# Four-byte key transposes, a lighter PE share, a reordered end and longer weight rows in a decode attention kernel

## The chip, the cores and the metric

The kernel runs on one core of a Trainium2 chip. The metric is the device time of one launch in microseconds (us), the median of several runs. Engines are named as in the profile: PE is TensorE (matmul), PEld its weight load, DVE VectorE, ACT ScalarE, SP SyncE, which here only issues DMA. The profile counts 16 DMA engines for the core. "Late engines" below means eight of them, which fall behind the other eight in the course of the run (in the kernel before all sixteen are within 0.6 us at the first load and the two groups some 20 us apart at the end, by the landing marks explained below).

## The reference, cut to what matters

One token passes through attention over a cache of 32768 keys in each of 32 heads of 192 elements, and then through a small MLP. K and V are 403 MB each in bf16. Every byte is used once, so a kernel that is limited only by loading would show nothing but loads.

```python
B, Sq, D = 1, 1, 640
H, Sk, Dh = 32, 32768, 192
...
def reference(A_x, A_k_cache, A_v_cache, A_wq, A_wo, B_x, B_w1, B_w2):
    def _A_ref(x, k_cache, v_cache, wq, wo):
        q = (x @ wq).reshape(B, Sq, H, Dh)                    # (transpose left out)
        scores = jnp.einsum("bhqd,bhkd->bhqk", q, k_cache) * (Dh ** -0.5)
        p = _softmax(scores, axis=-1)
        o = jnp.einsum("bhqk,bhkd->bhqd", p, v_cache)
        return o.reshape(B, Sq, H * Dh) @ wo                  # (transpose left out)
    ...
    h = x + _A_ref(_layernorm(x, axis=-1), A_k_cache, A_v_cache, A_wq, A_wo)
    h2 = h + _B_ref(_layernorm(h, axis=-1), B_w1, B_w2)       # w2 after relu after w1
    return h2
```

## The kernel before

A load brings 64 keys to each of the 128 partitions (3 MB) and is worked in two chunks of 32 keys a partition. Of each chunk, PE scores 20 keys: it transposes them in blocks of 128 bf16 columns, ACT copies the result out of PSUM, and PE multiplies. DVE scores the other 12 with a multiplication and a sum.

```python
full = [(JL, [(J, 20), (J, 20)])] * (Sk // (P * JL))      # JL = 64, J = 32: (keys of a chunk, those that PE scores)
ends = full[:-1] + [(40, [(20, 12), (20, 12)]), (16, [(16, 10)]), (8, [(8, 4)])]   # the last head
...
def transposes(g):
    ...
    for b0 in range(0, NB, 8):
        nb = min(8, NB - b0)
        tp = tps.tile([P, 8, P], bf16, name="tp")
        for b in range(nb):
            off = (c0 + jc - jp) * Dh + (b0 + b) * P
            nc.tensor.transpose(out=tp[:, b, :], in_=kt[:, off:off + P], identity=ident_b[:])   # L239
        nc.scalar.copy(out=kT[:, b0:b0 + nb, :], in_=tp[:, 0:nb, :])                            # L240

def scores_pe(g):          # three matmuls for two keys
    ...
    for i in range(JP // 2):
        nc.tensor.matmul(sp[:, 2 * i:2 * i + 2], lhsT=kT[:, 3 * i + 1, :], rhs=qm[:, 1:3], ...)     # L249
        nc.tensor.matmul(sp[:, 2 * i:2 * i + 1], lhsT=kT[:, 3 * i, :], rhs=qm[:, 0:1], ...)         # L251
        nc.tensor.matmul(sp[:, 2 * i + 1:2 * i + 2], lhsT=kT[:, 3 * i + 2, :], rhs=qm[:, 3:4], ...) # L253

def scores_dve(g):
    ...
    nc.vector.tensor_tensor(out=pr[:, 0:JD, :], in0=kt[...], in1=qb[...], op=A.mult)                # L266
    nc.vector.reduce_sum(out=sc[:, 0:JD], in_=pr[:, 0:JD, :], axis=mybir.AxisListType.X)            # L269
...
# the loop: PE's program order
for g in range(G):
    ...                    # loads of this chunk
    transposes(g)
    if g > 0:
        pv(g - 1)          # the matmuls with V, L293
    scores_pe(g)
    sc = scores_dve(g)
    ...
    exp_dve(g, sc)
den_mm(H - 1)
den_rec(H - 1)
pv(G - 1)
o_scale(H - 1)             # L314 on DVE, L315 on ACT
o_turn(H - 1)              # L327: o by columns, for the projection
project(H // 2 - 1)        # with wo; then layernorm and MLP
```

The softmax here doesn't subtract the row's maximum and nothing guards it: scores larger than these inputs give would overflow.

## Time and profile before

The time is 1954.15 us (1954.13 to 1954.15 in the three runs).

| what | before | where it stands |
|---|---|---|
| span of the profiled run | 1952.3 us | first line of the page |
| DMA engines busy | 99.0% on the data queue | page, part 3 |
| rate in the middle | 429 to 431 GB/s | page, part 2 |
| PE / DVE / ACT busy | 82 / 69 / 55% | page, part 1 |
| instruction packets of queue q8 | 159 | page, part 3 |
| last full K load landed | 1912.1 us | landing marks in the trace |
| last matmul with V ended | 1940.66 us | chain in order of time |

The groups that the change rewrites are these three of part 5. The columns are line, engine, operation, output from input, count, then busy time and mean ns of one, then the idle time ahead of them and its main cause:

```profile
L266 DVE TENSOR_TENSOR pr<-kt,qb 128x2304 f32<-128x2304 bf16 (+1 forms) x258 | 655.0, 2539 | 483.3 <-DMA kt<-in_A_k_cache_dram 479.9
L239 PE MATMUL tp<-ident_b,kt 128*128 128x128 bf16 x7677 | 599.3, 242 | 342.8 <-DMA kt<-in_A_k_cache_dram 269.7
L269 DVE TENSOR_REDUCE sc<-pr 128x12 f32<-128x2304 f32 (+1 forms) x258 | 654.3, 2536 | 27.6 <-ACT kT L240 1.4
```

DVE waits 480 us for K loads and PE 270. That is the picture of a kernel that is limited by its DMA: time taken off a group of 600 us on PE need not save a microsecond.

The other quantity used throughout is not on the page. Each load leaves 16 landing marks in the trace, which I read as one for each DMA engine (the marks carry no engine's number). These are the marks of the last full K load of the kernel before, in us relative to the last of them at 1912.1:

```
-21.7 -21.7 -21.7 -21.5 -21.5 -21.4 -20.4 -17.5 | -1.8 -1.6 -1.5 -1.5 -1.5 -0.5 -0.2 0.0
```

Eight engines are 20 us ahead of the other eight. A load is whole only with the last mark (DVE began on this K at 1912.17, after 4.36 us of waiting for it), so the eight late ones set the pace. Below, "late mean" is the mean of the eight later marks of the last full V load, which follows that K: 1918.5 us before.

### The profile page before, as it was taken

To read this page: it belongs to the slowest core of one execution; us is meant where nothing else is said; L and a number is where in the kernel's file an instruction comes from. 1 tells how busy PE (TensorE), PEld (TensorE's weight loads), DVE (VectorE), ACT (ScalarE), POOL (GpSimd) and SP (SyncE) were. 2 spreads that over 40 slices of the span, in tenths; PEclk is the share of its full clock that TensorE was granted. 3 is DMA by queue.
4 is the path that set the end of the run, shared out by engine and by line. 5 is a ranking of instruction groups with operands and counts; after the bars stand their busy time and mean duration, and the time that the engine had idled before them with its cause. 6 is when DMAs were issued, how large, how long until landed. Compare 5 with 4: busy or idle time off the path is not lost.

```text
span 1952.3 us, 44906 instructions
## 1 busy us (share of the span) xinstructions
PE 1594.4 (82%) x20392; PEld 1122.4 (57%) x20392; DVE 1338.0 (69%) x654; ACT 1067.5 (55%) x2223; POOL 0.7 (0%) x6
## 2 busy tenths in 40 slices
PE   6887887878788788787888877888788887887887
PEld 4655565555556556555555655655555565565655
DVE  5766777667666676676767666777666766676675
ACT  4555555555555555555655555555555555555554
POOL 0000000000000000000000000000000000000000
PEclk9989889989998889998988989899899989898998
DMA  9999999999999999999999999999999999999996
GB/s 405 431 429 429 430 431 430 429 429 431 431 430 428 430 431 430 431 429 431 430 429 430 429 431 430 430 431 424 431 431 428 425 421 431 427 430 426 430 421 253
DMA packets 51522, 827.85 MB, mean 424 GB/s; under 512 B 4612, under 2 KB 17412, under 8 KB 18564
## 3 DMA queue, kind: packets, MB, share of 16 engines
q1 hardware_dynamic: 51332, 824.99, 99.0%
q8 instruction: 159, 2.61, 0.5%
q14 instruction: 31, 0.25, 0.0%
HBM read 824.97 MB, written 0.00 MB: 423 GB/s over the span
## 4 chain that ended last, share of the span: by engine, by line
DMA 77%; PE 17%; ACT 4%; DVE 1%; issue 1%; SPq 0%; ACTq 0%
DMA kt<-in_A_k_cache_dram 75%; PE o_ps L293 8%; PE tp L239 6%; ACT kT L240 3%; DMA vt<-in_A_v_cache_dram 1%; DVE pr L266 1%; PE sp L249 1%; PE sp L253 1%; PE sp L251 1%; PE qps L205 0%; ACT pA L276 0%; ACT pB L256 0%; DVE o_pair L314 0%; PE oT_ps L327 0%; ACT row_e L208 0%
## 5 line engine op out<-in xcount | busy, mean ns | idle before, releaser
L240 ACT COPY kT<-tp 128x1024 bf16<-128x1024 bf16 (+1 forms) x1025 | 905.2, 966 | 343.1 <-PE tp L239 340.2
L266 DVE TENSOR_TENSOR pr<-kt,qb 128x2304 f32<-128x2304 bf16 (+1 forms) x258 | 655.0, 2539 | 483.3 <-DMA kt<-in_A_k_cache_dram 479.9
L239 PE MATMUL tp<-ident_b,kt 128*128 128x128 bf16 x7677 | 599.3, 242 | 342.8 <-DMA kt<-in_A_k_cache_dram 269.7
L239 PEld LDWEIGHTS <-kt 128*128 128x128 bf16 x7677 | 531.1, 110 | 381.2 <-DMA kt<-in_A_k_cache_dram 280.2
L269 DVE TENSOR_REDUCE sc<-pr 128x12 f32<-128x2304 f32 (+1 forms) x258 | 654.3, 2536 | 27.6 <-ACT kT L240 1.4
L293 PE MATMUL o_ps<-vt,pB 128*2 128x384 bf16 x2559 | 498.8, 346 | 2.6 <-DMA vt<-in_A_v_cache_dram 2.6
L293 PEld LDWEIGHTS <-pB 128*2 128x2 bf16 x2559 | 203.8, 87 | 226.9 <-issue 65.9
L256 ACT ACTIVATE pB<-sp 128x20 bf16<-128x20 f32 (+1 forms) x258 | 48.4, 188 | 492.4 <-PE sp L253 492.4
L293 PE MATMUL o_ps<-vt,pA 128*2 128x384 bf16 x1537 | 291.9, 326 | 0.0
L249 PEld LDWEIGHTS <-kT 128*128 128x128 bf16 x2559 | 196.1, 96 | 85.7 <-issue 84.7
L249 PE MATMUL sp<-qm,kT 128*128 128x2 bf16 x2559 | 218.6, 164 | 0.5 <-ACT kT L240 0.5
L251 PE MATMUL sp<-qm,kT 128*128 128x1 bf16 x2559 | 215.0, 163 | 0.0
L253 PE MATMUL sp<-qm,kT 128*128 128x1 bf16 x2559 | 215.0, 163 | 0.0
L251 PEld LDWEIGHTS <-kT 128*128 128x128 bf16 x2559 | 198.7, 96 | 0.0
L293 PEld LDWEIGHTS <-pA 128*2 128x2 bf16 x1537 | 129.1, 84 | 120.8
L253 PEld LDWEIGHTS <-kT 128*128 128x128 bf16 x2559 | 197.4, 96 | 0.0
L276 ACT ACTIVATE pA<-sc 128x12 bf16<-128x12 f32 (+1 forms) x258 | 52.8, 205 | 0.0
L256 ACT ACTIVATION_READ_ACCUMULATOR pB<-sp 128x1 f32 x258 | 50.1, 194 | 0.0
L276 ACT ACTIVATION_READ_ACCUMULATOR pA<-sc 128x1 f32 x258 | 49.3, 191 | 0.0
L305 DVE TENSOR_REDUCE rec<-den 128x1 f32<-128x20 f32 x32 | 5.7, 179 | 60.2 <-PE den L299 60.2
L315 ACT ACTIVATE o_pair<-o_ps,rec 2x192 f32<-2x192 f32 x32 | 13.2, 412 | 26.9 <-DVE o_pair L314 26.9
L327 PE MATMUL oT_ps<-ident_f,o_pair 2*128 2x1 f32 x192 | 24.2, 247 | 0.1
(60 smaller groups left out, 191.4 us busy)
## 6 DMA issues: line engine op xcount, KB each, us to landing
kt<-in_A_k_cache_dram SPq DMA_DIRECT2D x127, 3072.0 KB, 35.7
vt<-in_A_v_cache_dram SPq DMA_DIRECT2D x127, 3072.0 KB, 31.4
wq<-in_A_wq_dram SPq DMA_DIRECT2D x8, 960.0 KB, 34.7
wo<-in_A_wo_dram SPq DMA_DIRECT2D x16, 480.0 KB, 31.2
kt<-in_A_k_cache_dram SPq DMA_DIRECT2D x1, 1920.0 KB, 30.7
vt<-in_A_v_cache_dram SPq DMA_DIRECT2D x1, 1920.0 KB, 25.4
kt<-in_B_w_dram SPq DMA_DIRECT2D x1, 1920.0 KB, 17.1
vt<-in_B_w_dram SPq DMA_DIRECT2D x2, 960.0 KB, 13.3
```

Of the source, the lines that this page charges most:

```text
L239: nc.tensor.transpose(out=tp[:, b, :], in_=kt[:, off:off + P], identity=ident_b[:])
L240: nc.scalar.copy(out=kT[:, b0:b0 + nb, :], in_=tp[:, 0:nb, :])
L249: nc.tensor.matmul(sp[:, 2 * i:2 * i + 2], lhsT=kT[:, 3 * i + 1, :], rhs=qm[:, 1:3], start=True, stop=False, skip_group_check=True)
L251: nc.tensor.matmul(sp[:, 2 * i:2 * i + 1], lhsT=kT[:, 3 * i, :], rhs=qm[:, 0:1], start=False, stop=False, skip_group_check=True)
L253: nc.tensor.matmul(sp[:, 2 * i + 1:2 * i + 2], lhsT=kT[:, 3 * i + 2, :], rhs=qm[:, 3:4], start=False, stop=True, skip_group_check=True)
L256: nc.scalar.activation(out=pB[:, 0:JP], in_=sp[:, 0:JP], func=F.Exp, scale=SCALE, accum_out=dsums[:, h, 2 * c + 1:2 * c + 2])
L266: nc.vector.tensor_tensor(out=pr[:, 0:JD, :], in0=kt[:, c0 * Dh:(c0 + JD) * Dh].rearrange("p (j d) -> p j d", d=Dh), in1=qb[:].unsqueeze(1 ...
L269: nc.vector.reduce_sum(out=sc[:, 0:JD], in_=pr[:, 0:JD, :], axis=mybir.AxisListType.X)
L276: nc.scalar.activation(out=pA[:, 0:JD], in_=sc[:, 0:JD], func=F.Exp, scale=SCALE, accum_out=dsums[:, h, 2 * c:2 * c + 1])
L293: nc.tensor.matmul(o[:], lhsT=p, rhs=vt[:, (c0 + j) * Dh:(c0 + j + 2) * Dh], start=first, stop=last)
L315: nc.scalar.activation(out=dst[:, 1, n0:n0 + Dh], in_=o[:, Dh:2 * Dh], func=F.Copy, scale=s[0:2, 1:2])
L327: nc.tensor.matmul(ps[:, b:b + 1], lhsT=src[:, i, b * P:(b + 1) * P], rhs=ident_f[0:2, i:i + 1], start=(i == 0), stop=(i == 1))
```

## The change

The intent has four parts. (1) Two neighbouring bf16 elements are taken as one 4-byte word, so that one transpose moves 256 columns; the scores then use every second element of the transposed block as weights, even and odd parity in turn. (2) PE scores 20 and 16 keys of the two chunks in turns, and DVE 12 and 16. (3) At the end all K pieces are scored ahead of the V work that waits for data. (4) The rows of wo are loaded as 3840 B instead of 1280 B, and o is written in a permuted order to suit. Cut to its core:

```diff
-    full = [(JL, [(J, 20), (J, 20)])] * (Sk // (P * JL))
-    ends = full[:-1] + [(40, [(20, 12), (20, 12)]), (16, [(16, 10)]), (8, [(8, 4)])]
+    full = [(JL, [(J, 20), (J, 16)])] * (Sk // (P * JL))
+    ends = full[:-1] + [(40, [(20, 12), (20, 12)]), (16, [(16, 8)]), (8, [(8, 4)])]
...
-    wo_view = A_wo.rearrange("(b p) n -> p b n", p=P)
+    wo_view = A_wo.rearrange("(g p b) n -> g p b n", p=P, b=3)
...          # V pieces of the end: one DMA for each chunk; qm of 12 columns, by block and parity
-                tp = tps.tile([P, 8, P], bf16, name="tp")
+                tp = tps.tile([P, 4, P], f32, name="tp")
                 for b in range(nb):
-                    off = (c0 + jc - jp) * Dh + (b0 + b) * P
-                    nc.tensor.transpose(out=tp[:, b, :], in_=kt[:, off:off + P], identity=ident_b[:])
-                nc.scalar.copy(out=kT[:, b0:b0 + nb, :], in_=tp[:, 0:nb, :])
+                    off = (c0 + jc - jp) * Dh + (b0 + b) * 2 * P
+                    nc.tensor.transpose(out=tp[:, b, :], in_=kt[:, off:off + 2 * P].bitcast(f32), identity=ident_f[:])
+                nc.scalar.copy(out=kT[:, b0:b0 + nb, :], in_=tp[:, 0:nb, :].bitcast(bf16))
...
-            for i in range(JP // 2):
-                ...                                            # three matmuls for two keys
+            for i in range(JP // 4):
+                for b in range(3):
+                    for e in range(2):
+                        nc.tensor.matmul(sp[:, 4 * i + b:4 * i + b + 2], lhsT=kT[:, 3 * i + b, e:2 * P:2],
+                                         rhs=qm[:, 4 * b + 2 * e:4 * b + 2 * e + 2], ...)
...          # scores_dve: more than 12 keys are done in pieces
+            n = -(-JD // JDM)
+            for j0, j1 in [(JD * i // n, JD * (i + 1) // n) for i in range(n)]:
...          # o_scale: the same two instructions with a permuted output
+            dst = o_pair[(h // 2) % 2][:].rearrange("q i (b p) -> q i p b", b=3)
+            nc.vector.tensor_scalar_mul(out=dst[:, 0, p0:p1, :], in0=src[:, 0], scalar1=s[0:2, 1:2])
+            nc.scalar.activation(out=dst[:, 1, p0:p1, :], in_=src[:, 1], func=F.Copy, scale=s[0:2, 1:2])
...          # the end, behind the loop over the full chunks
+        transposes(ENDS[0])
+        pv(ENDS[0] - 1)
+        sc = scores_dve(ENDS[0])
+        for i, g in enumerate(ENDS[1:]):
+            transposes(g)
+            scores_pe(g - 1)
+            exp_dve(g - 1, sc)
+            sc = scores_dve(g)
+            if i > 0:
+                pv(g - 2)
+        scores_pe(G - 1)
+        exp_dve(G - 1, sc)
         den_mm(H - 1)
         den_rec(H - 1)
+        pv(G - 2)
         pv(G - 1)
```

More of the change, by code (lines that the diff above doesn't have):

```diff
@@ L65 @@
     G = len(chunks)
+    ENDS = [g for g in range(G) if chunks[g][2] >= len(loads) - NEND]
     NCH = [sum(1 for q in chunks if q[0] == h) for h in range(H)]
     NCM = max(NCH)
-    NBM = max(q[5] for q in chunks) * Dh // P
-    JDM = max(q[4] - q[5] for q in chunks)
+    NBM = max(q[5] for q in chunks) * Dh // (2 * P)
+    JDM = 12
     const = ctx.enter_context(tc.tile_pool(name="const", bufs=1))
@@ L79 @@
     scp = ctx.enter_context(tc.tile_pool(name="scp", bufs=3))
-    pcp = ctx.enter_context(tc.tile_pool(name="pcp", bufs=3))
+    pcp = ctx.enter_context(tc.tile_pool(name="pcp", bufs=6))
     small = ctx.enter_context(tc.tile_pool(name="small", bufs=2))
@@ L112, in load_wo, with load_part @@
         t = wop.tile([P, 3, D], bf16, name="wo")
-        nc.sync.dma_start(out=t[:], in_=wo_view[:, 3 * pr:3 * pr + 3, :])
+        nc.sync.dma_start(out=t[:], in_=wo_view[pr])
         wo_t[pr] = t
-    def load_part(ld, src, pool, tag, name):
+    def load_part(ld, src, pool, tag, name, parts=None):
         h, k0, jl = loads[ld]
@@ L122, in load_part @@
         t = pool.tile([P, size], bf16, tag=tag, name=name)
-        nc.sync.dma_start(out=t[:, 0:jl * Dh], in_=src[h, k0:k0 + P * jl, :].rearrange("(p j) d -> p (j d)", p=P))
+        rows = src[h, k0:k0 + P * jl, :].rearrange("(p j) d -> p (j d)", p=P)
+        for j0, j1 in parts or [(0, jl)]:
+            nc.sync.dma_start(out=t[:, j0 * Dh:j1 * Dh], in_=rows[:, j0 * Dh:j1 * Dh])
         return t
@@ L129, in load_v @@
     def load_v(ld):
-        vt_t[ld] = load_part(ld, v_hd, vpool, "vt", "vt")
+        parts = [(q[3], q[3] + q[4]) for q in chunks if q[2] == ld] if ld >= len(loads) - NEND else None
+        vt_t[ld] = load_part(ld, v_hd, vpool, "vt", "vt", parts)
     w_t = {}
@@ L157 @@
     nc.vector.memset(eps_t[:], eps)
-    rows_e = [const.tile([1, 4 * P], bf16, name=f"row_e{i}") for i in range(2)]
+    rows_e = [const.tile([1, 3 * Dh], bf16, name=f"row_e{i}") for i in range(2)]
     for r in rows_e:
@@ L207, in q_rows @@
             r = rows_e[h % 2]
-            nc.scalar.copy(out=r[0:1, 0:Dh], in_=qps[:])
-            nc.scalar.copy(out=r[0:1, 4 * P - Dh:4 * P], in_=qps[:])
+            nc.scalar.copy(out=r[0:1, Dh:2 * Dh], in_=qps[:])
         def q_spread(h):
             r = rows_e[h % 2]
-            qbps = mm_bank([P, Dh + 4], f32, "qbps")
-            nc.tensor.matmul(qbps[:, 0:Dh], lhsT=ones_row[:], rhs=r[0:1, 0:Dh], start=True, stop=True)
-            for i in range(4):
-                nc.tensor.matmul(qbps[:, Dh + i:Dh + i + 1], lhsT=r[0:1, i * P:(i + 1) * P],
-                                 rhs=ones_row[0:1, 0:1], start=True, stop=True)
+            qbps = mm_bank([P, Dh + 12], f32, "qbps")
+            nc.tensor.matmul(qbps[:, 0:Dh], lhsT=ones_row[:], rhs=r[0:1, Dh:2 * Dh], start=True, stop=True)
+            i = Dh
+            for b in range(3):
+                for e in range(2):
+                    for off in ((1 - 0) * Dh + b * (2 * P - Dh), b * (2 * P - Dh)):
+                        nc.tensor.matmul(qbps[:, i:i + 1], lhsT=r[0:1, off + e:off + 2 * P:2],
+                                         rhs=ones_row[0:1, 0:1], start=True, stop=True)
+                        i += 1
             qb = qbp.tile([P, Dh], bf16, name="qb")
             nc.scalar.copy(out=qb[:], in_=qbps[:, 0:Dh])
-            qm = qbp.tile([P, 4], bf16, name="qm")
-            nc.scalar.copy(out=qm[:], in_=qbps[:, Dh:Dh + 4])
+            qm = qbp.tile([P, 12], bf16, name="qm")
+            nc.scalar.copy(out=qm[:], in_=qbps[:, Dh:Dh + 12])
             qb_t[h], qm_t[h] = qb, qm
@@ L231, in transposes @@
             kt = kt_t[ld]
-            NB = jp * Dh // P
-            kT = tsb.tile([P, NBM, P], bf16, name="kT")
-            for b0 in range(0, NB, 8):
-                nb = min(8, NB - b0)
-                tp = tps.tile([P, 8, P], bf16, name="tp")
+            NB = jp * Dh // (2 * P)
+            kT = tsb.tile([P, NBM, 2 * P], bf16, name="kT")
+            for b0 in range(0, NB, 4):
+                nb = min(4, NB - b0)
+                tp = tps.tile([P, 4, P], f32, name="tp")
                 for b in range(nb):
-                    off = (c0 + jc - jp) * Dh + (b0 + b) * P
-                    nc.tensor.transpose(out=tp[:, b, :], in_=kt[:, off:off + P], identity=ident_b[:])
-                nc.scalar.copy(out=kT[:, b0:b0 + nb, :], in_=tp[:, 0:nb, :])
+                    off = (c0 + jc - jp) * Dh + (b0 + b) * 2 * P
+                    nc.tensor.transpose(out=tp[:, b, :], in_=kt[:, off:off + 2 * P].bitcast(f32), identity=ident_f[:])
+                nc.scalar.copy(out=kT[:, b0:b0 + nb, :], in_=tp[:, 0:nb, :].bitcast(bf16))
             kT_t[g] = kT
@@ L247, in scores_pe @@
             sp = sps.tile([P, J], f32, name="sp")
-            for i in range(JP // 2):
-                nc.tensor.matmul(sp[:, 2 * i:2 * i + 2], lhsT=kT[:, 3 * i + 1, :], rhs=qm[:, 1:3],
-                                 start=True, stop=False, skip_group_check=True)
-                nc.tensor.matmul(sp[:, 2 * i:2 * i + 1], lhsT=kT[:, 3 * i, :], rhs=qm[:, 0:1],
-                                 start=False, stop=False, skip_group_check=True)
-                nc.tensor.matmul(sp[:, 2 * i + 1:2 * i + 2], lhsT=kT[:, 3 * i + 2, :], rhs=qm[:, 3:4],
-                                 start=False, stop=True, skip_group_check=True)
+            for i in range(JP // 4):
+                for b in range(3):
+                    for e in range(2):
+                        nc.tensor.matmul(sp[:, 4 * i + b:4 * i + b + 2], lhsT=kT[:, 3 * i + b, e:2 * P:2],
+                                         rhs=qm[:, 4 * b + 2 * e:4 * b + 2 * e + 2],
+                                         start=(i == 0 and b == 0 and e == 0),
+                                         stop=(i == JP // 4 - 1 and b == 2 and e == 1), skip_group_check=True)
             pB = pcp.tile([P, J], bf16, name="pB")
@@ L264, in scores_dve @@
             qb = qb_t[h]
-            pr = prp.tile([P, JDM, Dh], f32, name="pr")
-            nc.vector.tensor_tensor(out=pr[:, 0:JD, :], in0=kt[:, c0 * Dh:(c0 + JD) * Dh].rearrange("p (j d) -> p j d", d=Dh),
-                                    in1=qb[:].unsqueeze(1).to_broadcast([P, JD, Dh]), op=A.mult)
             sc = scp.tile([P, J], f32, name="sc")
-            nc.vector.reduce_sum(out=sc[:, 0:JD], in_=pr[:, 0:JD, :], axis=mybir.AxisListType.X)
+            n = -(-JD // JDM)
+            for j0, j1 in [(JD * i // n, JD * (i + 1) // n) for i in range(n)]:
+                pr = prp.tile([P, JDM, Dh], f32, name="pr")
+                nc.vector.tensor_tensor(out=pr[:, 0:j1 - j0, :],
+                                        in0=kt[:, (c0 + j0) * Dh:(c0 + j1) * Dh].rearrange("p (j d) -> p j d", d=Dh),
+                                        in1=qb[:].unsqueeze(1).to_broadcast([P, j1 - j0, Dh]), op=A.mult)
+                nc.vector.reduce_sum(out=sc[:, j0:j1], in_=pr[:, 0:j1 - j0, :], axis=mybir.AxisListType.X)
             return sc
@@ L311, in o_scale @@
             o = o_t.pop(h)
-            dst = o_pair[(h // 2) % 2]
-            n0 = (h % 2) * Dh
-            nc.vector.tensor_scalar_mul(out=dst[:, 0, n0:n0 + Dh], in0=o[:, 0:Dh], scalar1=s[0:2, 1:2])
-            nc.scalar.activation(out=dst[:, 1, n0:n0 + Dh], in_=o[:, Dh:2 * Dh], func=F.Copy, scale=s[0:2, 1:2])
+            dst = o_pair[(h // 2) % 2][:].rearrange("q i (b p) -> q i p b", b=3)
+            p0, p1 = (h % 2) * Dh // 3, (h % 2 + 1) * Dh // 3
+            src = o[:].rearrange("q (i p b) -> q i p b", i=2, b=3)
+            nc.vector.tensor_scalar_mul(out=dst[:, 0, p0:p1, :], in0=src[:, 0], scalar1=s[0:2, 1:2])
+            nc.scalar.activation(out=dst[:, 1, p0:p1, :], in_=src[:, 1], func=F.Copy, scale=s[0:2, 1:2])
         oT_t = {}
@@ L344 @@
         q_spread(0)
-        for g in range(G):
+        for g in range(ENDS[0]):
             h, c, ld, c0, jc, jp = chunks[g]
-            end = ld - (len(loads) - NEND)
-            if end == 0 and c0 == 0:
-                for i in range(NEND):
-                    load_k(ld + i)
-                for i in range(NEND):
-                    load_v(ld + i)
-                load_w("w1", B_w1, kpool, "kt", 1)
-                load_w("w2", B_w2, vpool, "vt", 2)
-            elif end < 0 and c0 == 0 and g > 0:
+            if c0 == 0 and g > 0:
                 load_k(ld)
@@ L380 @@
             exp_dve(g, sc)
+        for ld in range(len(loads) - NEND, len(loads)):
+            load_k(ld)
+        for ld in range(len(loads) - NEND, len(loads)):
+            load_v(ld)
+        load_w("w1", B_w1, kpool, "kt", 1)
+        load_w("w2", B_w2, vpool, "vt", 2)
+        transposes(ENDS[0])
[10 more added lines that the diff above has]
+        exp_dve(G - 1, sc)
         den_mm(H - 1)
         den_rec(H - 1)
+        pv(G - 2)
         pv(G - 1)
```

## The prediction

> **What bounds the kernel now.** I read the page first: parts 1 to 3, then the chain of part 4.
>
> ```profile
> span 1952.3 us, 44906 instructions
> PE 1594.4 (82%) x20392; PEld 1122.4 (57%) x20392; DVE 1338.0 (69%) x654; ACT 1067.5 (55%) x2223; POOL 0.7 (0%) x6
> ...
> q1 hardware_dynamic: 51332, 824.99, 99.0%
> q8 instruction: 159, 2.61, 0.5%
> ...
> DMA 77%; PE 17%; ACT 4%; DVE 1%; issue 1%; SPq 0%; ACTq 0%
> DMA kt<-in_A_k_cache_dram 75%; PE o_ps L293 8%; PE tp L239 6%; ACT kT L240 3%; DMA vt<-in_A_v_cache_dram 1%; DVE pr L266 1%; PE sp L249 1%; PE sp L253 1%; PE sp L251 1%; PE qps L205 0%; ACT pA L276 0%; ACT pB L256 0%; DVE o_pair L314 0%; PE oT_ps L327 0%; ACT row_e L208 0%
> ```
>
> The reader is to see that the 16 DMA engines are busy for the whole span, that no compute engine is, and that the chain is mostly K loads. A pair of loads (K and V, 6.29 MB) takes 14.6 us at the 431 GB/s of the middle slices; PE is busy 12.2 us of it, DVE 10.4. So nearly all the compute that the change touches is hidden.
>
> The share of 99% hides one thing. The trace also holds the 16 landing marks of each load, one per DMA engine. Sorted, they fall into two groups of eight: the first load lands within 0.6 us, the one that is whole at 882 us has eight engines 13 us ahead, from 1400 us on about 20 us ahead. Up to 1250 us the gap between the two groups grows by 0.175 us for each packet of the queue "instruction" (a straight-line fit of the gap against the count of such packets). The reading that fits is that instruction fetches run on the late eight engines only, and one 16 KB fetch costs its engine 8 x 0.175 = 1.4 us (the packet itself took 0.93 us). The 159 fetches then cost 27.8 us, and they are on the path: a load has landed only when its late engines have. [...]
>
> Next the end, from the chain in order of time and the DVE timeline:
>
> ```profile
> 1906.10 25.42 DMA vt<-in_A_v_cache_dram
> ...
> 1939.51 0.40 PE den L299 x2
> 1939.91 0.75 PE o_ps L293 x4
> 1940.68 0.42 DVE o_pair L314
> ...
> 1949.51 0.39 PE ytp L408
> ```
>
> ```profile
> 1912.17 2.56 DVE L266 TENSOR_TENSOR pr<-kt,qb 128x2304 f32<-128x2304 bf16 x1 [4.36 <-DMA kt<-in_A_k_cache_dram]
> 1914.83 2.55 DVE L269 TENSOR_REDUCE sc<-pr 128x12 f32<-128x2304 f32 x1
> ...
> 1924.21 1.76 DVE L266 TENSOR_TENSOR pr<-kt,qb 128x1536 f32<-128x1536 bf16 x1 [1.57 <-DMA kt<-in_A_k_cache_dram]
> 1926.07 1.75 DVE L269 TENSOR_REDUCE sc<-pr 128x8 f32<-128x1536 f32 x1
> ...
> 1935.42 0.95 DVE L269 TENSOR_REDUCE sc<-pr 128x4 f32<-128x768 f32 x1
> ```
>
> The first V of the end lands at 1931.5. Until then PE stands at L293, in program order, with scores behind it that need no V; 9.2 us of PE work follow to the end of the last L293 at 1940.66, and 11.6 us of projection and MLP follow that. By the landing marks the late engines never pause: last full K 1912.1, its V 1919.4, end K pieces 1924.1 to 1927, V 1931.5 to 1934.4, w1 1939.1, w2 1944.0.
>
> [...] the one f32 transpose (L408, 128 columns) is one pass of 0.38 us, begun at 1949.51 at a half clock and read by DVE at 1949.92[...] f32 loads of 128 columns take 187 ns and start 0.11 us apart, bf16 ones 0.056 us apart among the transposes.
>
> **The change, part by part.**
>
> *Transposes.* 7677 bf16 become 3456 f32 (half as many blocks, 18 PE keys in place of 20 on average). For a pair: before 60 x 0.056 = 3.4 us, after 27 x 0.112 to 0.17 = 3.0 to 4.6 us. *Scores*: 54 matmuls for 60; with every second word as weights I take 25 to 50 ns each, 1.4 to 2.7 us against 1.5. *L293* is unchanged, 32 x 0.163 = 5.2 us. PE comes to 10 to 13 us of 14.6. *ACT*: seven copies of 128x1024 at 1.015 and 0.82-like remainders, 6.9 us for 7.7. *DVE*: a 20-key chunk keeps 12 keys (2.56 + 2.55 us); a 16-key chunk has 16 in two pieces of 8 (2 x (1.76 + 1.75) = 7.0). A pair is 12.1 us for 10.2, near 12.6 with gaps. All of it lies beside 14.6 us of DMA. K buffers come free 2 us later, but at that moment the late engines still have about 24 us queued (V, K and V of later loads). So the steady part gets nothing from faster compute, and loses nothing.
>
> *Fetches.* PE instructions, counted from the built program with each f32 transpose as a load and a matmul: 31324 for 40784. 31324 / 256 = 122 packets for 159; 37 x 0.175 = 6.5 us off the late engines. This is on the path. (Were a transpose one instruction in the fetched program, 51 packets and 8.9 us.)
>
> *wo.* Each engine takes 8 rows of 3840 B in place of 24 of 1280 B. In the trace 1280 B took 56.9 ns and 3072 B 124.3 ns; on that slope 3840 B is 153 ns, an estimate. 24 x 56.9 - 8 x 153 = 142 ns, x 16 loads = 2.3 us, on the path.
>
> So the last full K lands at 1912.1 - 8.6 = 1903.5 (6.35 us of fetches by then, 2.3 of wo).
>
> *The end.* The new order puts all scores ahead of the PV that wait. The V pieces would then land at 1922.7 to 1925.6, w1 at 1930.3, w2 at 1935.2. But now the DVE is what is late. From 1903.5: one 12-key chunk 5.25 us, one of 16 keys 7.3, three of 8 keys 3.65 each, one of 4 keys 2.0 (durations of the timeline above, with its gaps) = 25.5, so the last L269 ends at 1929.0. Then exp 0.45, den 0.40, PV of the last two pieces (8 + 4 matmuls, 1.3 + 0.7, since both stand behind den in the new program) = 1931.9, and the 11.6 us after the last PV as before: span 1943.5. w2 is needed near 1939.6 and is there at 1935.2. The measured time is 1.85 us over the span (1954.15 to 1952.3), so **1945.3 us**, 0.45% less. Of the 8.8 us, 8.6 are DMA work taken off the late engines; the pipelined end brings only 0.2 net, as the DVE chain from the last full K (40.0 us) is as long as the old one (40.2 us): the new DVE share eats what the new order gives. If the DVE chain were no matter, w2 at 1935.2 plus 3.9 us would give 1939.1 (1941.0 measured).
>
> **Rivals.**
> *The fetches do not matter* (the lag has another cause): only wo is left, about 1952. Against it: 91 fetches and 15.6 us of growing gap run along a line.
> *PE becomes the bound.* [...]
> *DVE becomes the bound.* Where a head changes, DVE waits for den some 2.9 us (1887.98 to 1890.91 in the timeline), so that one pair in four takes about 15.5 us against 14.6. The neighbours have 2 us of slack each, so I expect it absorbed; if not, up to 1 us a head, 1970 at worst.
> *The end gains more*: fetches at 51 packets and a shorter DVE chain, 1938 to 1940.
>
> **Range and chances.** The sum is 1945.3. The fetch count and the end's order can bring 3 to 9 us more; a DVE chain that starts late, or a fetch saving that is half as large, 3 to 6 us less. So 1937 to 1952 should hold it 8 times in 10. Over 2% faster would need 39 us, which no part holds[...], 1%. Over 2% slower is the PE rival, 4%.
>
> **What would show each step right or wrong.** Right: PE near 31300 / 2 matmuls, some 122 packets on the instruction queue, the packets under 2 KB fewer by 6144, the chain still mostly kt loads in the middle; L248 near 0.11 to 0.17 us apart; DVE near 1580 us busy; the landing gap growing more slowly; at the end DVE without a pause from the last full K, and the last L281 near 1929. Wrong: DMA slices under 425 GB/s in the middle with SP waiting for PE or DVE on every load (a compute engine is the bound); as many fetches as before; the last L305 held by V rather than by DVE.

Cut out of this text, where it is marked, are rules and figures of the hardware that no trace of this case shows. No term of the sum is cut: 6.35 us of fetches and 2.3 of wo bring the last full K to 1903.5, the end as written brings the span to 1943.5, and 1.85 more make the 1945.3 us. What stands behind the terms is this:

- The 256 in "31324 / 256" is what the trace before shows: 159 packets of 16 KB for 40784 PE and PEld instructions, 256.5 for each packet.
- That fetches run on the late engines only is the prediction's reading, and 1.4 us for one fetch an estimate from the slope of the gap. The packet records name no engine.
- The 24 and 8 rows of an engine are in the traces: where each packet is put behind the one that ends as it starts (to within 10 ns), those of a wo load form 16 chains: of 24 packets of 1280 B before, with no packet left over in 5 of the 16 loads, and of 8 packets of 3840 B after, in 10 of 16. In the other loads the sort is not clean.
- The upper values of 0.17 us for a transpose and 50 ns for a score are assumptions. Measured in the trace before were 0.11 us from one f32 load of 128 columns to the next, and 25 ns from one score to the next.
- The 1% and the 4% are estimates. The first rests on the terms and on the measured rate (most of the middle slices held 428 to 431 GB/s before); behind the second, the rival in which PE becomes the bound, no figure is left.

## The result

The changed kernel took 1947.24 us, the median of four runs (1946.0 to 1948.44), beside 1954.15 us. The ratio is 0.9964, with a 95% interval of 0.9947 to 0.9982: some 7 us, or 0.4%, and within 2%. The runs of several kernels sit at two levels some 2 us apart (of the changed kernel 1946.0 and 1946.1, then 1948.4 and 1948.4); both are counted, and why there are two is open. The four runs of the kernel before were all at its lower level, so level for level the gain is 8.1 us. Profiles that are compared below fell at or near the lower level, except that of the wo experiment.

The page of the kernel after, parts 1, 3 and 4:

```profile
span 1944.4 us, 35685 instructions
PE 1595.2 (82%) x15662; PEld 1096.0 (56%) x15662; DVE 1582.1 (81%) x908; ACT 985.3 (51%) x2064; POOL 0.7 (0%) x6
...
q1 hardware_dynamic: 47380, 824.99, 99.2%
q8 instruction: 123, 2.02, 0.4%
...
DMA 70%; DVE 20%; PE 8%; issue 1%; ACT 1%; SPq 0%; DVEq 0%; ACTq 0%
```

DMA is as busy as before and DVE has gone from 69% to 81%, yet no compute engine has become the bound. PE executes 9460 instructions less (PE and PEld together 31324 for 40784), at nearly the same busy time. (The mean granted clock of PE was 0.858 here and 0.911 before, so PE's busy times are not at one clock.) The queue "instruction" q8 has 36 packets less. Part 5, the groups that answer to the three of before:

```profile
L278 DVE TENSOR_TENSOR pr<-kt,qb 128x1536 f32<-128x1536 bf16 (+1 forms) x385 | 777.1, 2018 | 244.5 <-DMA kt<-in_A_k_cache_dram 236.0
...
L248 PE MATMUL tp<-ident_f,kt 128*128 128x128 f32 x3456 | 585.6, 336 | 331.9 <-DMA kt<-in_A_k_cache_dram 320.4
L281 DVE TENSOR_REDUCE sc<-pr 128x8 f32<-128x1536 f32 (+1 forms) x385 | 775.8, 2015 | 31.6 <-DVE pr L278 0.9
```

Half as many transposes fill the same busy time, since one 4-byte transpose takes about twice as long: their starts in the trace are 0.109 us apart (1903.641, 1903.750, 1903.859), against 0.056 before. Both hold at the full clock; where the granted clock was halved the medians are 0.213 and 0.107. DVE still waits 236 us for K, so it has slack left.

The end on DVE, from its timeline (start, duration, instruction; in brackets idle time and what ended it):

```profile
1903.46 2.56 DVE L278 TENSOR_TENSOR pr<-kt,qb 128x2304 f32<-128x2304 bf16 x1 [1.39 <-DMA kt<-in_A_k_cache_dram]
...
1926.89 0.96 DVE L278 TENSOR_TENSOR pr<-kt,qb 128x768 f32<-128x768 bf16 x1
1927.95 0.95 DVE L281 TENSOR_REDUCE sc<-pr 128x4 f32<-128x768 f32 x1
```

And the chain that ends last, in order of time (start, duration, step; den is the matmul that sums the denominator of the softmax, which the scaling of o needs):

```profile
1928.94 0.31 ACT pA L288 x2
1929.25 0.04 issue
1929.29 0.40 PE den L311 x2
1929.69 2.05 PE o_ps L305 x12
1931.77 0.54 DVE o_pair L328
1932.33 0.59 ACT o_pair L329
1932.92 0.04 issue
1932.97 1.28 PE oT_ps L341 x10
...
1941.46 0.39 PE ytp L433
```

The landing marks of the last full K load, as those of the kernel before were shown, are these (relative to 1903.4):

```
-19.0 -18.9 -18.9 -18.2 -18.1 -17.8 -13.1 -10.9 | -1.4 -0.4 -0.2 -0.2 -0.1 -0.1 -0.0 0.0
```

The gap between the groups is smaller. Two of the early engines have fallen behind as well, so the groups are not quite uniform.

The three stretches of the span add up to the difference. The last full K load lands at 1903.4 for 1912.1, -8.7. From there to the end of the last matmul with V it is 28.4 us for 28.6, -0.2. From there to the end of the span it is 12.6 us for 11.7, +0.9. The sum is -8.0, and the spans differ by as much (7.9 on the pages, by rounding). So the gain is made while DMA is running, the new end gives almost nothing, and the tail takes one microsecond back. The end is not compared at one clock: the granted clock was halved from 1910.4 to 1917.2 us in the kernel before, and nowhere between the last full K and den in the changed one.

### The profile page after: what moved, and what is told of

It is laid out like the page before. It is cut to its first block, busy times and chain, and to the rows that moved or that the text cites. A ratio compares the mean times of both kernels' runs of the same rounds, so it can differ in the third digit from the quotient of the medians.

```text
span 1944.4 us, 35685 instructions
## 1 busy us (share of the span) xinstructions
PE 1595.2 (82%) x15662; PEld 1096.0 (56%) x15662; DVE 1582.1 (81%) x908; ACT 985.3 (51%) x2064; POOL 0.7 (0%) x6
## 4 chain that ended last, share of the span: by engine, by line
DMA 70%; DVE 20%; PE 8%; issue 1%; ACT 1%; SPq 0%; DVEq 0%; ACTq 0%
DMA kt<-in_A_k_cache_dram 69%; DVE pr L278 11%; DVE sc L281 8%; PE o_ps L305 4%; PE tp L248 3%; DMA vt<-in_A_v_cache_dram 1%; PE sp L260 1%; DVE o_pair L328 0%; ACT kT L249 0%; PE den L311 0%; DVE rec L317 0%; DVE rec L318 0%; PE yps L427 0%; PE h1ps L420 0%; DVEq L281 0%
## 5 line engine op out<-in xcount | busy, mean ns | idle before, releaser
L278 DVE TENSOR_TENSOR pr<-kt,qb 128x1536 f32<-128x1536 bf16 (+1 forms) x385 | 777.1, 2018 | 244.5 <-DMA kt<-in_A_k_cache_dram 236.0
L249 ACT COPY kT<-tp 128x1024 bf16<-128x1024 bf16 (+1 forms) x898 | 816.5, 988 | 291.1 <-PE tp L248 282.9
L248 PE MATMUL tp<-ident_f,kt 128*128 128x128 f32 x3456 | 585.6, 336 | 331.9 <-DMA kt<-in_A_k_cache_dram 320.4
L281 DVE TENSOR_REDUCE sc<-pr 128x8 f32<-128x1536 f32 (+1 forms) x385 | 775.8, 2015 | 31.6 <-DVE pr L278 0.9
L248 PEld LDWEIGHTS tp<-ident_f,kt 128*128 128x128 f32 x3456 | 508.1, 176 | 354.7 <-issue 322.5
L305 PE MATMUL o_ps<-vt,pA 128*2 128x384 bf16 x1792 | 336.1, 328 | 0.0
L265 ACT ACTIVATE pB<-sp 128x20 bf16<-128x20 f32 (+2 forms) x258 | 48.0, 186 | 478.6 <-PE sp L260 478.6
L260 PEld LDWEIGHTS <-kT 128*128 128x128 bf16 x6912 | 192.5, 97 | 85.0 <-issue 83.9
L305 PEld LDWEIGHTS <-pA 128*2 128x2 bf16 x1792 | 152.3, 85 | 147.2 <-issue 9.8
L288 ACT ACTIVATE pA<-sc 128x12 bf16<-128x12 f32 (+2 forms) x258 | 54.4, 211 | 127.7 <-DVE sc L281 127.6
L341 PE MATMUL oT_ps<-ident_f,o_pair 2*128 2x1 f32 x192 | 24.1, 247 | 0.9 <-DVE o_pair L328 0.6
L341 PEld LDWEIGHTS oT_ps<-ident_f,o_pair 2*128 2x128 f32 x192 | 22.6, 186 | 1.6 <-DVE o_pair L328 1.0
```

Source lines behind the costliest of these rows:

```text
L248: nc.tensor.transpose(out=tp[:, b, :], in_=kt[:, off:off + 2 * P].bitcast(f32), identity=ident_f[:])
L249: nc.scalar.copy(out=kT[:, b0:b0 + nb, :], in_=tp[:, 0:nb, :].bitcast(bf16))
L260: nc.tensor.matmul(sp[:, 4 * i + b:4 * i + b + 2], lhsT=kT[:, 3 * i + b, e:2 * P:2], rhs=qm[:, 4 * b + 2 * e:4 * b + 2 * e + 2], start=(i ...
L265: nc.scalar.activation(out=pB[:, 0:JP], in_=sp[:, 0:JP], func=F.Exp, scale=SCALE, accum_out=dsums[:, h, 2 * c + 1:2 * c + 2])
L278: nc.vector.tensor_tensor(out=pr[:, 0:j1 - j0, :], in0=kt[:, (c0 + j0) * Dh:(c0 + j1) * Dh].rearrange("p (j d) -> p j d", d=Dh), in1=qb[:] ...
L281: nc.vector.reduce_sum(out=sc[:, j0:j1], in_=pr[:, 0:j1 - j0, :], axis=mybir.AxisListType.X)
```

## The experiments

The theory, to be tested here, is that instruction fetches load the eight late DMA engines and that a load waits for them: each fetch costs 0.175 us of the path, and the gain is the fetches that were saved, with a little from wo. The first rival is that fewer fetches only go along with something else in PE's work. For the end, the theory was that DVE alone is late there. All kernels below gave correct results. Those of one session share their runs of the kernel before, whose median was 1954.65 (a0, e4, e5, e6), 1954.76 (e1, e2, e3, e8), 1954.53 (e7, e9, e10) and 1954.31 (e11). "e" numbers are the first part of each label.

### a0_after_again: the changed kernel unaltered, for comparison

> The changed kernel once more, so that the next three have it on their own chip. It had two levels so far, 1946.1 and 1948.4, beside 1954.15 of the kernel before; I expect 1946 to 1948.5, 123 packets on the instruction queue and the last full K landed near 1903.4.

1946.44 us (ratio 0.9959, 0.9946 to 0.9971), span 1944.5, 123 packets, late mean 1910.5: as before, so the result repeats. It is the base of e4, e5 and e6.

### e4_more_fetch: the fetches put back without the old work

```diff
             sp = sps.tile([P, J], f32, name="sp")
+            for i in range(18):
+                nc.tensor.matmul(sp[:, 0:1], lhsT=kT[:, 0, 0:2 * P:2], rhs=qm[:, 0:1],
+                                 start=True, stop=True, skip_group_check=True)
```

> The changed kernel with 18 more one-column matmuls at the head of each chunk's scores (4644 in all, their results overwritten): 9288 more PE instructions, no more data, 0.45 us of PE work a chunk. Theory (eight DMA engines carry the PE's program, and set the end): 36 more packets on the instruction queue, 159 in all, the landing gap growing again by 0.175 us a packet, the last full K 6.1 us later, and the time 6.3 us longer than the changed kernel beside it. Rival (the fetches do not matter): 36 more packets and a time within 0.7 us of the changed kernel.

It took 1954.12 us (ratio 0.9999, 0.9986 to 1.0013), which is the time of the kernel before. Part 3 of its page:

```profile
q8 instruction: 159, 2.61, 0.5%
```

Dummy matmuls of one column, whose results are overwritten, bring back exactly the 159 packets. The late mean went from 1910.5 to 1916.7, +6.2, for 36 x 0.175 = 6.3 that the theory gave. The time rose by 7.7 and not 6.3; the remaining 1.4 fell after the last full loads, where PE has more to do as well and, unlike in a0, ran at the half clock from 1911.6 to 1915.0 us.

### e5_more_pe_time: more PE time with few instructions

```diff
-            sp = sps.tile([P, J], f32, name="sp")
+            sp = sps.tile([P, 512], f32, name="sp")
+            for i in range(2):
+                nc.tensor.matmul(sp[:], lhsT=kT[:, 0, 0:2 * P:2], rhs=kt_t[ld][:, 0:512],
+                                 start=True, stop=True, skip_group_check=True)
```

> Control for the run before: the changed kernel with two 512-column matmuls at the head of each chunk's scores, so 0.43 us of PE work a chunk, as much as the 18 small ones, but only 1032 more PE instructions. Theory: 4 more packets, 0.7 us longer than the changed kernel. Rival (it is the PE time that counts): as much longer as the run with 18 small matmuls, some 6 us if that one is.

This is the control for e4. It took 1948.09 us, 1.65 more than a0 by the medians (0.85 by the means, as both have two levels), where 0.7 was expected. Parts 1 and 3 of its page:

```profile
PE 1636.0 (84%) x16178; PEld 1085.9 (56%) x16178; DVE 1582.1 (81%) x908; ACT 983.2 (51%) x2064; POOL 0.7 (0%) x6
...
q8 instruction: 127, 2.08, 0.4%
```

The late mean is 1911.1: +0.6, where four more packets make 0.7. The rest fell at the end, where the large matmuls stand in PE's way. The control is not as even as planned: PE's busy time grew by 51 us over a0's 1584.7, and by 91 in e4 (1675.6), and the granted clocks differ (0.914, 0.866 and 0.887). But more than half of e4's PE time moved the loads by a tenth as much. So it is the number of instructions and not PE's time that moves the loads. Together e4 and e5 refute the first rival. The dose was applied in one direction only, but e2 and e7 below take instructions away and lie on the same line: the gap between the medians of the two groups of engines, fitted against the fetches up to 1250 us, has slopes of 0.174 to 0.177 us in the twelve profiles from before to e11 without e8 and e9 (159, 132, 131, 127 and 123 packets). With the means of the groups it is 0.155 to 0.162, since some of the early eight fall behind too. The firm figure is e4's, which needs no groups of early engines: 6.2 us for 36 packets, 0.17 each.

What the 1.4 us of one fetch may consist of can be seen in the packet records (1.4 is an estimate from the slope of 0.175, times 8 if the late engines share the fetches evenly, which no record shows). A 16 KB packet took 0.93 us itself. Of the 123 in the kernel after, 115 ended within 0.1 us of the start of a 24 KB data packet that took 1.3 us or more instead of 0.91; as many moments thrown at random over the run met such a start one or two times. In the kernel before it was 152 of 159. Packets over 1 us took 0.47 us more than the usual one in the mean, and 0.93 + 0.47 = 1.40. The records do not name the DMA engine of a packet, so this match is suggestive and not a proof.

### e2_f32_only: the 4-byte transposes and parity scores alone

```diff
-    full = [(JL, [(J, 20), (J, 16)])] * (Sk // (P * JL))
+    full = [(JL, [(J, 20), (J, 20)])] * (Sk // (P * JL))
 # against the changed kernel; wo, o_scale, V pieces and the order of the end as before
```

> The kernel before with only the transposes as 4-byte words and the scores by parity, 20 keys of each chunk on PE throughout (the end pieces 12, 12, 8, 4), old wo, old end. PE instructions 33600, so 131 to 132 packets for 159. Theory: the last full K 27 x 0.175 = 4.7 us earlier, the same chain after it, 4.7 us less than the kernel before: near 1949.5. Rival (fetches do not matter): within 0.5 us of the kernel before.

1949.77 us (ratio 0.9976, 0.9963 to 0.9988), 5.0 less than before. With 132 packets, 27 less, the late mean is 1913.4, -5.1 (27 x 0.175 = 4.7). PE's busy time did not fall (1609 us for 1594, at a mean clock of 0.912 for 0.911); the format pays because it needs fewer instructions.

### e7_jp20: the changed kernel with 20 and 20 PE keys

```diff
-    full = [(JL, [(J, 20), (J, 16)])] * (Sk // (P * JL))
+    full = [(JL, [(J, 20), (J, 20)])] * (Sk // (P * JL))
```

> The changed kernel with 20 keys of each chunk on PE throughout in place of 20 and 16 in turns. Theory: 132 instruction packets for 123, so the last full K 1.6 us later; after it the DVE chain is 2 us shorter but PE has three transposes and six scores more, and PE is as late there as DVE, so nothing is won back: 1.5 to 2 us over the changed kernel. Rival (DVE share is what counts): 0.5 us under it or better.

1948.48 us (ratio 0.997, 0.9957 to 0.9982), 6.05 under its session's before where a0 is 8.2 under. It has 131 packets, and its late mean of 1912.2 is 1.7 after that of a0. So handing four keys of every second chunk to DVE is worth about 2 us, of which the 1.7 at the loads is the firm part (the two times are of different sessions, and the intervals of the ratios overlap). DVE takes 1.9 us for four keys, but they no longer cost PE instructions.

### e1_wo_only: the wo rows alone

```diff
-    wo_view = A_wo.rearrange("(b p) n -> p b n", p=P)
+    wo_view = A_wo.rearrange("(g p b) n -> g p b n", p=P, b=3)
 # against the kernel before; with the load and o_scale of the changed kernel
```

> The kernel before with only the wo part: rows of 3840 B and the permuted places in o_scale. Theory: 4096 fewer packets, 142 ns less a load on each engine, so the last full K 2.3 us earlier than in the kernel before (1909.8 for 1912.1); the permuted writes of o_scale, which the changed kernel showed 0.13 us (DVE) and 0.18 us (ACT) slower, cost 0.3 us at the end and let fewer of the 12 small matmuls start early (0.4 us): 1.6 us less in all, near 1952.5. Still 159 instruction packets. Rival (the change's whole gain is here): 7 to 8 us less.

1954.32 us beside 1954.76 (ratio 0.9999, 0.9986 to 1.0011): no gain in the time. The late mean is 1917.3, -1.2 and not -2.3. I had taken 56.9 ns for a 1280 B packet, a mean that included the rows of w2, and had not reckoned with the overlap of neighbours. Without w2 the mean is 55.3 ns, a 3840 B packet took 150, and packets start some 3.5 ns before the one ahead has ended (24 KB packets take 912 ns and start 908 apart). Then 24 x (55.3 - 3.5) - 8 x (150 - 3.5) = 71 ns, and 16 loads give 1.1 us.

The rest went at the end. o_scale writes with a stride and takes 0.54 and 0.59 us for 0.42 and 0.42. Ten small matmuls (L341) instead of six stand behind the ACT half, since each block of 128 permuted columns now holds a part of the last head: 1.28 us for 0.84. Its profile is also the one at the upper level, so the time itself says only that the two roughly cancel. e11 settles that.

### e3_end_only: the new order of the end alone

```diff
 # against the kernel before: V pieces by chunk, the end loop of the changed kernel
         den_mm(H - 1)
         den_rec(H - 1)
+        pv(G - 2)
         pv(G - 1)
```

> The kernel before with only the new order of the end. Last full K unchanged at 1912.1, 159 instruction packets. If the end were DVE alone: 22.6 us of DVE from there for 12, 12, 8, 8, 6 and 4 keys, then 2.9 us and the 11.6 us tail, 1949.1 of span, 3.1 us less than the kernel before. The run with a light DVE end has shown that PE is as late as DVE there (its PE ran without a pause from the last full K to the last PV, 28.8 us); by that the end here is 28 to 29 us to the last PV and no more than 0 to 1 us is gained.

1953.1 us beside 1954.76 (ratio 0.9992, 0.9978 to 1.0005, which includes no gain at all). The late mean is 1918.5, unmoved. From the last full K to the last matmul with V it is 27.4 us for 28.6. A gain of 1.2 to 1.7 us at most is far from the 3.1 that DVE's chain alone would have allowed, which speaks for PE being late as well. (The run that the expectation refers to is e6 below, which was made before this one. The granted clock was halved for 3.4 us here, from 1911.4, and for 6.8 in the kernel before; a part of the gain may be that.)

The parts add up where the loads are concerned: -1.2 (e1), -5.1 (e2), 0 (e3), -1.7 (e7 against after) make -8.0, and the late mean of the changed kernel moved from 1918.5 to 1910.5.

### e6_light_end: less for DVE at the end

```diff
-    ends = full[:-1] + [(40, [(20, 12), (20, 12)]), (16, [(16, 8)]), (8, [(8, 4)])]
+    ends = full[:-2] + [(JL, [(J, 20), (J, 20)])] + [(40, [(20, 16), (20, 16)]), (16, [(16, 12)]), (8, [(8, 4)])]
```

> The changed kernel with fewer keys on DVE at the very end: last full load 20 and 20 keys on PE, then 16, 16, 12 and 4 (DVE 12, 12, 4, 4, 4, 4 for 12, 16, 8, 8, 8, 4). Theory (the end is the DVE chain from the last full K): DVE needs 18.5 us for 25.5, its last reduction ends 7 us earlier, and then the last V piece (landed at 1927.3 in the changed kernel) sets the end: span near 1941.1 for 1944.4, 3.3 us less. Rival (the end is set by the last V or by w2 already): no shorter than the changed kernel by more than 0.5 us.

1946.82 us (ratio 0.9959, 0.9946 to 0.9971) and a span of 1945.0 for a0's 1944.5: no gain, where the theory of the prediction asked for 3.3 us. Its chain, in order of time:

```profile
1929.09 0.25 PE sp L260 x6
1929.36 0.27 ACT pB L265 x2
1929.63 0.19 ACT pA L288 x2
1929.82 0.04 issue
1929.86 0.40 PE den L311 x2
```

And the busy time of the engines between the last full K and den, for this kernel and then for the changed one (stretch, its length, PE, PEld, DVE, ACT, POOL, PE's clock, DMA share, GB/s):

```profile
1903.50:1929.30 25.80, 25.13 (x266) 16.81 (x266) 17.82 (x12) 17.87 (x40) 0.00 (x0) 0.93 0.94 362
```

```profile
1903.50:1929.30 25.80, 21.93 (x231) 14.28 (x231) 24.55 (x14) 15.80 (x40) 0.00 (x0) 1.00 0.89 343
```

In the changed kernel DVE is busy for 24.55 of 25.80 us and PE for 21.93. With the lighter DVE share DVE had finished its scores at 1925.13, but PE was busy for 25.13 us, and den had to wait for the scores of PE and the exponential behind them. The edit does not make DVE's keys vanish; it hands them to PE, which has little slack. What is refuted is that handing DVE's keys to PE would bring the 3.3 us. That den waits for DVE in the changed kernel is not refuted: e10 shows that it does. How much of PE's delay here is its keys is open, since PE's clock was halved from 1904.2 to 1907.6 us, which by the clock alone can have cost it up to 1.7 us (an estimate, half of 3.4), and was not halved at this place in the changed kernel.

### e10_pv_first: V matmuls that wait for nothing, ahead of den

```diff
         exp_dve(G - 1, sc)
+        pv(G - 2)
         den_mm(H - 1)
         den_rec(H - 1)
-        pv(G - 2)
         pv(G - 1)
```

> The changed kernel with the PV of the last but one piece ahead of den in the program. In the changed kernel PE stood from 1927.7 to 1929.3 for the last exp and then did den and 12 PV matmuls, 1.3 us of which (8) could have filled that wait. Theory: last PV at 1930.35 for 1931.74, 1.4 us less than the changed kernel, with the last exp (DVE) still what den waits for. Rival (PE has no slack there either): no change.

1944.93 us (1944.62 to 1945.31; ratio 0.995, 0.9939 to 0.9962), span 1943.0 for 1944.4. This is the fastest kernel, 1.5 us under a0's median, though in another session. Its chain at the place:

```profile
1929.34 0.40 PE den L311 x2
1929.74 0.75 PE o_ps L305 x4
1930.52 0.55 DVE o_pair L328
```

And PE's timeline at den, in the changed kernel and then here:

```profile
1929.29 0.40 PE L311 MATMUL den<-dsums,ones_mat 128*128 128x20 f32 x2 [1.65 <-ACT pA L288]
```

```profile
1929.34 0.40 PE L311 MATMUL den<-dsums,ones_mat 128*128 128x20 f32 x2 [0.40 <-ACT pA L288]
```

Four matmuls now follow den instead of twelve. In the changed kernel PE was idle for 1.65 us ahead of den, waiting for the exponential of DVE's last scores, with those eight matmuls behind den in its program; here it has 0.40. Den itself starts at the same time although PE has done 1.3 us more by then, so it is DVE's chain that den waits for. It is the same amount of work in a better order.

### e11_old_wo: e10 with the wo part undone

```diff
-    wo_view = A_wo.rearrange("(g p b) n -> g p b n", p=P, b=3)
+    wo_view = A_wo.rearrange("(b p) n -> p b n", p=P)
 # against e10; with the load and o_scale of the kernel before
```

> The kernel e10_pv_first with the wo part undone (rows of 1280 B in their old places, o_scale not permuted). Theory (wo is a wash): the late engines get 1.1 to 1.2 us later, so the last full K lands that much later (1904.5 to 1904.7 for 1903.4), and the tail after the last PV is 1.0 us shorter (about 11.6 us for 12.65): the time is within 0.5 us of e10_pv_first, 1944.5 to 1945.5, and the mean landing of the late eight at the last full V is about 1911.8. Rival (the wo part is worth the 2.3 us that the prediction gave it, and the longer tail has another cause): 1947 or more, with the tail still at 12.6.

1945.52 us (1945.31 to 1945.66; ratio 0.9953, 0.994 to 0.9967), span 1943.7 for 1943.0. The late mean is 1911.9, 1.2 after e10's, as expected. From the last matmul with V to the end it is 11.8 us for 12.5, so the permuted output costs 0.7 in the tail. The last matmul with V moved by 1.5, a little more than the loads, and the net worth of the wo part is about 0.6 us, which the intervals of the two ratios do not tell from nothing. The rival, 2.3 us, is refuted.

### e8_wo_eight: which engines are the late ones

```diff
-        nc.sync.dma_start(out=t[:], in_=wo_view[pr])
+        step = 8 if pr % 2 == 0 else P
+        for p0 in range(0, P, step):
+            nc.sync.dma_start(out=t[p0:p0 + step], in_=wo_view[pr][p0:p0 + step])
```

> The changed kernel with every second wo load issued as 16 DMAs of 8 partitions each. [...] Theory (eight fixed engines carry the fetches and set the pace): [...] the gap at the end shrinks from 20 us to some 2 us and the time falls by up to 9.6 us, to 1937; if they are the late ones, it rises by 9.6 us. Rival (the lag is not one of fixed engines, or does not set the pace): the time stays within 1 us of the changed kernel.

The intent was to move work from one group of engines to the other. The fall to 1937 stands for the case that the small DMAs run on the early engines, the rise for the case that they run on the late ones; both are estimates.

1988.78 us (ratio 1.0174), and the test is spoiled. SP's waits:

```profile
SPq L116 <- DMA vt<-in_A_v_cache_dram: 109.1, 16, 7.6
SPq L116 <- DMA kt<-in_A_k_cache_dram: 98.3, 15, 7.0
```

At 31 places a small DMA of the split wo load had to wait until an earlier K or V load had landed. For 207 us in all nothing new was queued, and the DMA engines ran dry: eight of the 40 slices fell to 369 to 386 GB/s. Engines that run dry catch up with each other (the marks of the V load ahead of the last split spread over 4.0 us, those of the K load behind it over 0.9), so the landing gap at the end no longer tells anything.

The marks at the splits do. Each small DMA left eight marks with its data and one some 0.5 us after its issue. At the five splits where the V load ahead shows two groups (near 263, 508, 754, 999 and 1245 us), the first small DMA has six of its eight marks with the early group and two with the late one. So by the marks the small DMAs ran on six early engines and two late ones there, and not on one of the two groups, which neither this test nor e9 had foreseen.

### e9_rows_moved: ten V loads cut in 112, 8 and 8 partitions

```diff
-                nc.sync.dma_start(out=t[:, j0 * Dh:j1 * Dh], in_=rows[:, j0 * Dh:j1 * Dh])
+            for p0, p1 in [(0, 112), (112, 120), (120, P)] if name == "vt" and ld < 120 and ld % 12 == 6 else [(0, P)]:
+                nc.sync.dma_start(out=t[p0:p1, j0 * Dh:j1 * Dh], in_=rows[p0:p1, j0 * Dh:j1 * Dh])
```

> A cleaner form of the run with wo on eight engines (there SP waited 207 us for old loads before it could issue the many small DMAs, which drained the queue). The changed kernel with ten of its V loads, spread over the run, issued as 112 + 8 + 8 partitions[...]; the bytes and all else stay. [...] Rival (the pace is set by the DMA engines together, so that only the sum of their work counts): within 1 us of the changed kernel.

Here too the engines on which the three parts would run, and the shift and the times worked out from that, are cut as not shown; the intent was that of e8.

2162.15 us (2152.52 to 2168.9; ratio 1.1058), 208 us over the kernel before, which neither side had foreseen. Part 2 of its page, the rate in 40 slices:

```profile
DMA  9999999999999999999998999999899999999995
GB/s 407 409 374 430 429 332 431 430 416 312 431 431 323 364 427 429 311 377 415 413 332 368 430 400 320 374 425 351 344 418 408 328 353 429 424 344 373 428 416 201
```

The engines stay busy while the rate falls. Between 100 and 120 us, for example, a 24 KB packet took 1.72 us in the mean, against 0.91 in the undisturbed stretches before it. SP also waited 102 us for V loads. The landing marks add what the page does not show: from the fourth split on (near 690 us) a single engine is 10 us or more behind the other fifteen, later some 25 us, and it is one of the eight that took the small DMAs, whose last marks are as late. So here one engine sets the pace. Why it falls behind, and why packets slow down so much around a split load, is open, and so is on which engines the fetches run.

## Why the prediction was right, and which of its terms were off

1945.3 us was predicted, with 1937 to 1952, and 1947.24 was measured (1946.44 in the repeat). The main mechanism held, by its own steps:

- *Fetches, 6.5 us on the path: right.* 36 packets were saved and not 37, so 6.3. e4 put them back and got 6.2 us back in the loads; e5 added PE time and did not. The saving in the format (e2) and in the key split (e7) both follow the count.
- *A steady part that neither gains nor loses by compute: right.* The rivals in which PE or DVE becomes the bound fell, and so did the one with 51 packets. Transposes ran 0.109 us apart at the full clock and 0.213 at the half one, where 0.112 to 0.17 was assumed, and DVE was busy for 1582 us where 1580 was predicted. The slices stayed at 428 to 432 GB/s in the middle.
- *wo, 2.3 us: mis-sized.* The term "24 x 56.9 - 8 x 153 = 142 ns" measured 71 ns by the packets, and 1.2 us at the late engines (e1, and e11 in the other direction).
- *Last full K at 1903.5: 1903.4 measured, partly by luck.* The late mean moved by 8.0 us and not 8.6. The last mark of this one load moved by 8.7, since marks scatter within a load.
- *"the 11.6 us after the last PV as before": wrong, 12.6.* The prediction read the diff of o_scale but not its cost, because it had counted that part only as a load. The strided writes and the four matmuls that moved behind ACT are in no term of its sum.
- *"But now the DVE is what is late": right for this program, but incomplete.* The last L281 ended at 1928.9 for a predicted 1929.0, and the last matmul with V at 1931.74 for 1931.9; e10 confirms that den waits for DVE. What the step left out is that PE is nearly as late, so that "If the DVE chain were no matter, ... 1939.1" was not to be had by handing keys to PE (e6).
- *"both stand behind den in the new program": right, 2.05 us for 2.0.* The prediction counted it and passed on; e10 shows that eight of those matmuls could be put into an idle stretch for 1.4 us of the span.
- *V pieces by 1925.6: late, without effect.* The last landed at 1927.3. Twelve matmuls ran after den at 1929.7 and none waited for V.
- *Fetches on the late engines: supported, not proved.* The packet records name no engine. What is shown is that the late marks move with the count of fetches (e4, 6.2 us for 36).

The predicted time is 1.1 to 1.9 us too low, and the tail accounts for 1.0 of it; the rest is about the two levels, for the lower one, 1946.1, is 0.8 above the prediction. The predicted span, 1943.5, was 0.9 under the measured one.

## What to carry to other kernels

In a kernel that is limited by DMA, count the instructions as a load of their own: here some 258 PE instructions brought one packet more and cost some 0.17 us of the path (e4: 9288, 36 and 6.2 us), although their work was hidden behind the loads. Look at the single landing marks before believing a mean of 99% (here eight of the 16 were 20 us behind). Where two engines are nearly equally late, look at what stands behind a wait in program order (e10) before moving work from one to the other (e6). And when a part shortens a load by permuting its rows, price what the permutation does to the serial tail behind it, for a microsecond there is worth as much as one in the loads (e1: 1.2 us earlier in the loads, and no gain in the time).
